# Clustered attention and feed-forward on one core: where transposes, signs, bounds and row sums are computed

## The chip, the core and the metric

The kernel runs on one core of a Trainium2 chip. A core has five engines with instruction queues of their own: TensorE (matrix products into PSUM; PE in the profile, with its weight loads as PEld), VectorE (DVE), ScalarE (ACT), GpSimd (POOL), and SyncE (SP), which issues the transfers of 16 DMA engines. SBUF is the working memory of 128 partitions, PSUM the memory that products are written to, which the kernel divides into named banks. The metric is the device time of one execution in microseconds.

## The reference

```python
def _attn_ref(q, k, v, centroids):            # q, k, v: 4 x 8 x 768 x 64, centroids 8 x 16 x 64
    q_assign = argmax of the cosine of each query with the 16 centroids of its head
    k_assign = the same for the keys
    mask = q_assign[:, :, :, None] == k_assign[:, :, None, :]
    scores = scale * np.matmul(q, k.transpose(0, 1, 3, 2))
    scores = np.where(mask, scores, -1000000000.0)
    scores = scores - np.max(scores, axis=-1, keepdims=True)
    attn = np.exp(scores)
    attn = attn / (np.sum(attn, axis=-1, keepdims=True) + 1e-09)
    return np.matmul(attn, v)

def _moe_ref(x, w_in, w_out):                 # 3072 x 512, 512 x 2048, 2048 x 512
    h = x @ w_in
    g = np.where(h >= 1, h, np.where(h <= -1, 0.0, (h + 1) ** 2 / 4))
    return g @ w_out
```

The attention output, its heads side by side, is the `x` of the second function. The two weight matrices come as 64-bit floats.

## The kernel before

Float32 accuracy is got from float16 products: an operand is scaled by a power of two and split into a high and a low float16 part, and three of the four products of parts are added up in PSUM.

**Attention.** Each of 4 batches has 4 pairs of heads. For a pair, `kv_load` brings k, q and v; `kv_scale` (line 526) reduces k and q to their largest absolute value per partition on VectorE, adds these up over the partitions on TensorE and derives powers of two from the sum (`to_scale`, line 500); `kq_split` (556) splits k and q into "natural" sets `kn` and `qn`, of which there are two each, and transposes them by DMA; `assign` (572) finds the nearest centroid of each row, writes the assignment as extra columns into the natural sets, and transposes them again, so that a product of the columns adds a penalty to scores of different clusters. The queries are taken in chunks of 256 (three a batch). For a chunk and a head pair there are four tiles of 128 queries by 768 keys (two heads j, two halves t). `at_scores` (705) computes a tile's scores into a PSUM bank and moves them to `sS` in one VectorE pass that also finds the row's bound. `at_soft` (735) takes the exponential on ScalarE, which adds up the rows into `rs`, casts the tile to float16, subtracts on GpSimd to get the low part, and sends both through one DMA transpose into `pT`; after the fourth tile `rr` becomes 1 / (sum + 1e-9). `at_av` (758) spreads `rr` over the partitions by four float32 products with an identity, multiplies the transposed tiles by v, and multiplies the two results on VectorE.

Before step 22 (`early()`, line 422) scores alternate between two banks, bank 0 for t = 0 and bank 1 for t = 1; later all are in bank 0, and bank 1 serves the feed-forward part.

**Feed-forward.** Each matrix comes in 8 blocks. `w_load` brings a block, `w_bits` (825) makes float32 out of the 64-bit words: absolute value of the high words on ScalarE, a shift on VectorE, then the low words' bits merged in (lines 849 to 851), then the sign bits (852 to 854). `w_sum` (858) bounds the block's column sums by TensorE, `w_split` (887) scales and splits. Fourteen of the sixteen blocks go through as one piece (`part is None`), two in halves. `ffn1` (900) and `ffn2` (925) run per chunk of 256 rows and block of 256 hidden columns, with the activation on VectorE and ScalarE between them; the cast and the low part of that activation go into `g`, a ring of two buffers.

**Order.** Nothing is issued directly. A recorder takes every operation with a step number, its price (`price`, line 75) and the memory regions it touches (`regions`, 54), simulates the five queues forward and backward for eight rounds, and issues the best order found. In the forward pass an engine may wait for a more urgent operation that becomes ready within `LOOK` times the cost of the one at hand, if it is more urgent by `MARGIN` (182). All recorded instructions have line 289 in the profile, so groups are told apart by tile: `w`, `wk` (weights), `kvq` (k, q, v and their transposes), `am` (bounds), `sS`, `hl`, `pT` (a score tile, its parts, its transpose), `rr`, `rs`, `banka` (products with v, and the spread rows).

Of the kernel before, what the change touches and what calls it, by code (L numbers as in the profile page):

```python
# [20 lines left out]


ONE, ES_MIN = 65504.0, 2.0**-23
EXP_MASK2 = 0x7F000000
TINY = 2.0**-47
W_TINY = 2.0**-90
# [2 lines left out]
LATENCY = dict(tensor=280, scalar=252, vector=230, gpsimd=175)  # L29
COLD, AHEAD = 75e3, 1500  # L30

LOOK, MARGIN = 1.0, 3000
ROUNDS = 8


# [1 line left out]
class Recorder:  # L37
# [15 lines left out]
    @staticmethod  # L53
    def regions(ap):
        if ap.space == bass.MemoryType.DRAM:
            return ap.tensor.name, [(0, 1, 0, 1)]
        size = mybir.dt.size(ap.dtype)
        (row, n), *free = ap.ap
        p0 = ap.start_partition()
        lo = (ap.offset - p0 * row) * size  # L60
        parts = [lo]
        if ap.space == PSUM and len(free) == 2:
            (st, k), *free = free
            parts = [lo + i * st * size for i in range(k)]
        size *= sum((k - 1) * st for st, k in free) + 1
        return ap.tensor.name, [(p0, p0 + n, x, x + size) for x in parts]
# [8 lines left out]
    def price(self, eng, op, out, ins, kw):  # L75

        if "dma" in op:
            n = 1
            for k in out.shape:
                n *= k  # L80
            kb = n * mybir.dt.size(out.dtype) / 1024

            return 33, 79.0 if kb == 2 else kb, "transpose" in op
        n = max(self.free(a) for a in [out] + ins[:1])
        ps = any(a.space == PSUM for a in ins)
        cols = sum(isinstance(kw.get(k), bass.AP) for k in ("scale", "bias", "scalar", "scalar1", "scalar2"))
        if eng == "tensor":
            n = self.free(ins[1])
            half = self.free(ins[0]) <= 64 and n > 100
            if ins[1].dtype == F32:  # L90
                n *= 4
            return n / 4.8 + 1.2 if half else max(n / 2.4 + 2.5, 24)
        if eng == "scalar":
            cols += kw.get("accum_out") is not None
            first = n == 1 and kw.get("scale") == 0.0
            return 93 + n / 1.2 + 94 * cols - 43 * ps + 1283 * first
        if eng == "vector":
            wide = [a for a in ins if self.free(a) > 1 or n == 1]
            wait = 400 if not ps and (len(wide) > 1 or op in ("tensor_scalar", "tensor_copy")) else 0
            fast = 1  # L100
            if op in ("tensor_scalar", "tensor_copy") and not ps:
                fast = 4 if mybir.dt.size(out.dtype) == 2 and mybir.dt.size(ins[0].dtype) == 2 and n > 64 else 2
            return 68 + n / 0.96 / fast + 61 * cols + 20 * (op == "reciprocal") + wait
        return 55 + n * (2.03 if op == "tensor_tensor" else 0.9 if op == "memset" else 3.5)
# [243 lines left out]
def tile_clustered_attention_moe(  # L348
# [10 lines left out]
    nc = tc.nc  # L359
# [50 lines left out]
    wk = tiles("wk", 2, 4096)  # L410
    rings["w32"], rings["x"] = Ring(wk[:1]), Ring(tiles("x", 3, 4096) + wk)

    wb = tiles("w", 1, 2 * NF * 4096)[0]
    raws = [wb[:, (2 * NF - n) * 1024 : (2 * NF - n + 2) * 1024] for n in (2, 4, 6)]
    bank = [psum.tile([P, 1024], F32, name=f"bank{i}") for i in range(3)]
# [21 lines left out]
    rings["c"] = Ring([rings["sS"].bufs[1][:, i * D : (i + 1) * D] for i in range(3)])  # L437
    rings["c_hl"] = Ring([rings["sS"].bufs[2]])
    make_identity(nc, idf)
    iota = const.tile([P, C], F32, name="iota")  # L440
    for c in range(C):
        nc.gpsimd.memset(iota[:, c : c + 1], float(C - c))
    zero = const.tile([P, 1], F32, name="zero")
    nc.gpsimd.memset(zero, 0.0)
    onh = const.tile([P, P], F16, name="onh")
    nc.gpsimd.memset(onh, 1.0)
    ones = const.tile([P, P], BF16, name="ones")
    nc.gpsimd.memset(ones, 1.0)
    cst = new("c", [D], F32)
# [68 lines left out]
    def kv_load(b, hp):  # L518
# [3 lines left out]
        for a, src, n in (("k", k, 1), ("q", q, 2), ("v", v, 3)):  # L522
            st = e[a] = view(e["parts"][n], [2, T * D], F32)
            rec.sync.dma_start(st, heads(src, b, hp))

    def kv_scale(b, hp):
        e = KV[b, hp]
        am = new("am", [2], BF16, 2)
        rec.vector.tensor_reduce(out=am, in_=e["kq"], op=ALU.max, axis=AX.X, apply_absolute_value=True)


        ar = misc(4)
        rec.tensor.matmul(ar[:, :2], ones, am, start=True, stop=True)
        sc = new("sc", [2], F32, 2)
        to_scale(ar[:, :2], sc)


        es, ph = new("es", [1], F32, 2), new("phi", [1], F32, 2)
        raw, ri = ar[:, 2:3], ar[:, 3:4]
        rec.vector.tensor_scalar(  # L540
            out=raw, in0=ar[:, 0:1], scalar1=ar[:, 1:2], scalar2=-QK, op0=ALU.mult, op1=ALU.mult
        )
        rec.vector.tensor_scalar(out=es, in0=raw, scalar1=-ES_MIN, scalar2=None, op0=ALU.min)
        rec.vector.reciprocal(ri, es)
        rec.vector.tensor_scalar(out=ph, in0=raw, scalar1=ri, scalar2=None, op0=ALU.mult)
        e.update(sc=sc, es=es, phi=ph)
# [9 lines left out]
    def kq_split(b, hp):  # L556

        e = KV[b, hp]
        for x, lower, at in (("k", 0, 0), ("q", 1, 4)):
            nat = e[x + "n"] = new(x + "n", [2 * T, 2, D], F16, 2)  # L560
            src = e[x].rearrange("p j (t d) -> p (j t) d", d=D)
            col = "kq".index(x)
            split(nat[:, :, 1 - lower], nat[:, :, lower], src, e["sc"][:, col : col + 1])
            e[x + "T"] = view(e["parts"][at], [2 * T, P], F16)
            transpose(e[x + "T"], nat)
# [6 lines left out]
    def assign(b, hp):  # L572
# [52 lines left out]
        pn = misc(2, C)  # L625
        with rec.group():
            for t in range(T):
                rec.tensor.matmul(pn, onh, kn[:, t::T, 0, :C], start=(t == 0), stop=(t == T - 1))
        has = new("has", [2, C], F32)
        rec.vector.tensor_scalar(out=has, in0=pn, scalar1=-ONE * (S - 0.5), scalar2=None, op0=ALU.is_gt)  # L630

# [73 lines left out]
    def at_scores(b, hp, c, j, t):  # L705
        e = KV[b, hp]
        n = j * CT + t
        pS = view(bank[n % 2 if early() else 0], [2, 512], F32)
        with rec.group():
            for a, (x, y) in enumerate((("qT", "kT"), ("q1", "k1"))):  # L710
                keys = e[y][:, j * T : (j + 1) * T].rearrange("p t q -> p (t q)")
                for h in range(2):
                    rec.tensor.matmul(
                        pS[:, h, :HS],
                        e[x][:, j * T + c * CT + t],
                        keys[:, h * HS : (h + 1) * HS],
                        start=(a == 0),
                        stop=(a == 1),
                    )
        sS = new("sS", [2, HS], F32, 3)  # L720
        bi = new("sbi", [1], F32, 4)

        rec.vector.tensor_tensor_reduce(
            out=sS,
            in0=pS[:, :, :HS],
            in1=zero.to_broadcast([P, S]),
            scale=e["er"][:, j * T + c * CT + t : j * T + c * CT + t + 1],
            scalar=3.0e38,
            op0=ALU.add,
            op1=ALU.min,  # L730
            accum_out=bi,
        )
        A[b, hp, c, j, t] = (sS, bi)

    def at_soft(b, hp, c, j, t):
        e = A.setdefault((b, hp, c), {})
        n = j * CT + t
        sS, bi = A.pop((b, hp, c, j, t))
        if n == 0:
            e["rs"] = new("rs", [4], F32, 4)  # L740
        if t == 0:
# [2 lines left out]
        rec.scalar.activation(  # L744
            out=sf, in_=sf, func=AF.Exp, bias=bi, scale=-1.0, accum_out=e["rs"][:, n : n + 1]
        )
        hl = new("hl", [2, S], F16, 3)
        rec.scalar.copy(hl[:, 0], sf)
        rec.gpsimd.tensor_tensor(out=hl[:, 1], in0=sf, in1=hl[:, 0], op=ALU.subtract)
        rec.sync.dma_start_transpose(out=e["pT", j][:, :, t, :], in_=hl.rearrange("p a s -> p (a s)"))  # L750
        if n == 3:

            rr = new("rr", [4], F32, 3)
            rec.scalar.activation(out=rr, in_=e["rs"], func=AF.Copy, bias=1e-9)
            rec.vector.reciprocal(rr, rr)
            e["rr"] = rr

    def at_av(b, hp, c):
        u = b * NCH + c
# [2 lines left out]
        pv, rb = bank_a[:, :CQ], bank_a[:, CQ:]  # L762
        with rec.group():
            for t in range(CT):
                for j in range(2):
                    rec.tensor.matmul(
                        rb[j * D : (j + 1) * D, t * P : (t + 1) * P],
                        e["rr"][:, j * CT + t : j * CT + t + 1].to_broadcast([P, D]),
                        idf,
                        start=True,  # L770
                        stop=True,
                    )
            for kc in range(T):
                for i, (va, pa) in enumerate(((0, 0), (0, 1), (1, 0))):
                    for j in range(2):
# [49 lines left out]
    def w_bits(a, f, part=None):  # L825
# [7 lines left out]
        if not w_wide:  # L833
# [15 lines left out]
        rec.vector.scalar_tensor_tensor(  # L849
            out=to, in0=lo, scalar=29, in1=t, op0=ALU.logical_shift_right, op1=ALU.bitwise_or  # L850
        )
        rec.vector.scalar_tensor_tensor(
            out=to, in0=hi, scalar=0x80000000, in1=to, op0=ALU.bitwise_and, op1=ALU.bitwise_or
        )
        if part is None:
            WL[a, f][1] = lo

    def w_sum(a, f, part):

# [27 lines left out]
    def w_split(a, f):  # L887
        t, tf = WL.pop((a, f))
        tf = tf.bitcast(F32)
        w = (w1 if a == 0 else w2)[f]  # L890
        whi, wlo = (w[:, x].rearrange("p a f -> p (a f)") for x in range(2))
        sw = WS.pop((a, f))
# [7 lines left out]
    def ffn1(u, f):  # L900
# [16 lines left out]
        rec.vector.tensor_scalar(out=r, in0=phf, scalar1=e["lo"], scalar2=e["hi"], op0=ALU.max, op1=ALU.min)  # L917
        rec.scalar.activation(out=r, in_=r, func=AF.Square, bias=e["ra"], scale=e["rs"])
        rec.vector.scalar_tensor_tensor(out=r, in0=phf, scalar=e["gs"], in1=r, op0=ALU.mult, op1=ALU.max)
        g = new("g", [2, 2 * CQ], F16, 2)  # L920
        rec.scalar.copy(g[:, 0], r)
        rec.gpsimd.tensor_tensor(out=g[:, 1], in0=r, in1=g[:, 0], op=ALU.subtract)
        F[u, f] = g
# [132 lines left out]
```

## Time and profile before

| | us |
|---|---|
| median of 3 runs | 966.27 |
| lowest, highest | 966.08, 966.28 |
| profiled execution, whole | 964.51 |
| its span, first to last instruction | 962.7 |

In the profile, busy time of an engine is the union of its instructions; idle time before an instruction is put down to whatever released it last. A row of a group reads: line, engine, operation, tile written, tiles read, shapes, count, then busy time, mean ns of one, and idle time with its releasers. In a row of the timeline the first number is the start, the second how long the merged instructions took, and the brackets hold the idle time before. A row of waits gives the total, how often, and the longest. The row of a window gives its length, then each engine's busy time with the number of instructions, the clock granted to TensorE, the DMA engines' share and GB/s.

### The profile page before, as it was taken

What the parts mean: (1) busy time and instruction counts of PE and PEld (TensorE: products, weight loads), DVE (VectorE), ACT (ScalarE), POOL (GpSimd) and SP (SyncE); (2) the same over time, 40 slices, a digit from 0 to 9 for tenths busy, and PEclk for the clock granted to TensorE, in tenths of its full rate; (3) what the DMA queues carried; (4) which work ended last, traced back from release to release, by engine and by line L of the source; (5) the groups of instructions that cost most, each with busy time, mean ns of one, the idle gap of its engine ahead of it and who ended that gap; (6) DMA issues with size and microseconds to landing.
All of it is one profiled execution on the core that took longest, in us unless ns stands there. A gap on an engine that the chain in (4) does not pass through costs nothing.

```text
span 962.7 us, 19220 instructions
## 1 busy us (share of the span) xinstructions
PE 824.1 (86%) x7348; PEld 567.2 (59%) x7348; DVE 639.8 (66%) x1341; ACT 654.8 (68%) x1095; POOL 551.2 (57%) x421
## 2 busy tenths in 40 slices
PE   0335547878999999998988999999989999999998
PEld 0223335555666766675656766776666757767664
DVE  6998986878689865556778665546986554454231
ACT  3676877775667877765767687757777677676332
POOL 1375777574555767663655667656655666656311
PEclk9999779989999999999999999999999999999999
DMA  9998787778589986876789878867999776566100
GB/s 279 263 202 195 175 207 161 164 175 194 125 176 178 169 141 117 170 148 142 173 154 198 145 156 152 166 130 159 209 192 154 139 132 122 108 118 110 34 22 22
DMA packets 426780, 148.68 MB, mean 154 GB/s; under 512 B 403520, under 2 KB 418880, under 8 KB 426688
## 3 DMA queue, kind: packets, MB, share of 16 engines
q1 hardware_dynamic: 426688, 147.46, 75.7%
q8 instruction: 57, 0.93, 0.4%
q14 instruction: 35, 0.29, 0.1%
HBM read 40.40 MB, written 6.29 MB: 49 GB/s over the span
## 4 chain that ended last, share of the span: by engine, by line
PE 67%; DVE 22%; issue 5%; ACT 2%; POOL 2%; DMA 1%; SPq 0%; ACTq 0%; DVEq 0%; POOLq 0%
PE bank L289 47%; PE banka L289 12%; PE bankh L289 9%; DVE w L289 4%; DVE sS L289 4%; DVE bank L289 2%; DVE r L289 2%; DVE wk L289 1%; DVE am L289 1%; DVE qn L289 1%; DVE kn L289 1%; POOL hl L289 1%; DVE kvq L289 1%; DVE mx L289 1%; DMA kvq<-in_v_dram 1%
## 5 line engine op out<-in xcount | busy, mean ns | idle before, releaser
L289 POOL TENSOR_TENSOR hl<-sS,hl 128x768 f16<-128x768 f32 x192 | 330.4, 1725 | 182.5 <-ACT hl L289 103.6
L289 PE MATMUL bank<-w,g 128*128 128x512 f16 x1152 | 273.1, 383 | 0.5 <-DVE o L289 0.5
L289 PEld LDWEIGHTS <-kvq 128*64 128x64 f16 (+1 forms) x3264 | 195.4, 107 | 128.3 <-issue 80.8
L289 PEld LDWEIGHTS <-w 128*128 128x128 f16 x2304 | 224.5, 98 | 66.7 <-issue 25.5
L289 DVE CUSTOM_DVE_ANT_0 sS<-bank,zero,er 128x768 f32<-128x768 f32 x192 | 194.2, 1012 | 93.1 <-PE bank L289 77.0
L289 ACT ACTIVATE sS<-sS,sbi 128x768 f32<-128x768 f32 x192 | 179.2, 933 | 98.8 <-DVE sbi L289 92.8
L289 PE MATMUL bank<-kvq 128*128 128x384 f16 x768 | 164.1, 338 | 47.5 <-DVE sbi L289 42.0
L289 POOL TENSOR_TENSOR g<-r,g 128x512 f16<-128x512 f32 x96 | 115.2, 1200 | 152.7 <-ACT g L289 139.5
L289 PEld LDWEIGHTS <-g 128*128 128x128 f16 x1152 | 111.0, 98 | 122.8 <-issue 10.1
L289 ACT CAST hl<-sS 128x768 f16<-128x768 f32 x192 | 157.4, 825 | 7.4 <-DMA pT<-hl 5.6
L289 PE MATMUL bank<-x,w 128*128 128x256 f16 x1032 | 125.6, 275 | 10.0 <-DVE r L289 4.4
L289 ACT ACTIVATE r<-r,f_ra,f_rs 128x512 f32<-128x512 f32 x96 | 77.8, 811 | 79.4 <-DVE r L289 74.7
L289 PE MATMUL banka<-pT,kvq 128*64 128x256 f16 x1728 | 108.0, 281 | 0.0
L289 DVE TENSOR_SCALAR r<-bank,f_lo,f_hi 128x512 f32<-128x512 f32 x64 | 51.7, 808 | 61.6 <-PE bank L289 45.4
L289 ACT CAST g<-r 128x512 f16<-128x512 f32 x96 | 58.8, 613 | 31.7 <-DVE r L289 24.8
L289 DVE SCALAR_TENSOR_TENSOR r<-bank,f_gs,r 128x512 f32<-128x512 f32 x64 | 48.0, 749 | 30.9 <-ACT r L289 18.7
L289 PE MATMUL bank<-wk,w 128*128 128x256 f16 x504 | 60.1, 272 | 5.9 <-DVE r L289 4.9
L289 PE MATMUL bankh<-x,w 128*128 128x256 f16 x504 | 59.9, 273 | 0.2 <-DVE es L289 0.2
L289 DVE TENSOR_SCALAR r<-bankh,f_lo,f_hi 128x512 f32<-128x512 f32 x32 | 25.9, 809 | 30.8 <-PE bankh L289 24.8
L289 PEld LDWEIGHTS <-ones 128*128 128x128 bf16 x148 | 13.9, 120 | 50.5 <-issue 46.7
L289 POOL TENSOR_TENSOR w<-w 128x1024 f16<-128x1024 f32 x14 | 31.5, 2252 | 14.7 <-ACT w L289 14.7
L289 PE MATMUL bank<-wk,ones 128*128 128x128 bf16 x116 | 13.2, 277 | 29.8 <-DVE wk L289 29.8
(135 smaller groups left out, 840.1 us busy)
## 6 DMA issues: line engine op xcount, KB each, us to landing
w<-in_moe_w_in_dram SPq DMA_DIRECT2D x14, 512.0 KB, 4.9
w<-in_moe_w_out_dram SPq DMA_DIRECT2D x14, 512.0 KB, 4.3
kvq<-in_k_dram SPq DMA_DIRECT2D x16, 384.0 KB, 4.0
kvq<-in_q_dram SPq DMA_DIRECT2D x16, 384.0 KB, 3.7
kvq<-in_v_dram SPq DMA_DIRECT2D x16, 384.0 KB, 4.1
out_dram<-o SPq DMA_DIRECT2D x11, 512.0 KB, 3.4
pT<-hl SPq DMA_TRANSPOSE x192, 4.1
o<-in_v_dram SPq DMA_DIRECT2D x8, 384.0 KB, 3.9
```

What stands on the lines that cost most here:

```text
L289: fn(*args, **kw)
```

## The change

- **First batch partly transposed by TensorE.** In `at_soft`, for tiles with t = 0 before step 22, the exponential's result stays float32, six TensorE transposes write it back into the tile's own score bank, ScalarE copies it to the high part in `pT`, and VectorE subtracts for the low part. The cast, GpSimd's subtraction and the DMA transpose of these tiles fall away.
- **Signs off VectorE.** For the 14 whole blocks the sign merge is replaced by ScalarE's `Sign` of the high words in place and a GpSimd multiplication in `w_split`.
- **Bounds off VectorE.** `kv_scale` sums squares on ScalarE (one `Square` with an accumulator for k, one for q) in place of the reduction for the largest absolute value; the squares themselves go into the natural set as scrap. The scale follows by halving the exponent.
- **Four natural sets** for the first batch: two of their own, one in two `x` buffers, one in the buffers of `g` and `o`; later batches alternate between the first two.
- **Rows of 1 / sum by float16 products.** `rr` is split in two float16 parts by two GpSimd operations of 4 columns, and `at_av` spreads it by eight float16 products with an identity scaled by 2^-10, in place of four float32 products.
- **Shorter waits.** `LOOK` falls from 1.0 to 0.4, `MARGIN` rises from 3000 to 4000 (ns); transposes get a price and PSUM regions of more dimensions are split.

```diff
+UNIT = 2.0**-10
-LOOK, MARGIN = 1.0, 3000
+LOOK, MARGIN = 0.4, 4000
...
-        if ap.space == PSUM and len(free) == 2:
+        if ap.space == PSUM and len(free) > 1:
...
+            if op == "transpose":
+                n *= 2
-            if ins[1].dtype == F32:
+            elif ins[1].dtype == F32:
                 n *= 4
...
+    gb = tiles("g", 1, 4096)[0]
+    rings["g"] = Ring([gb[:, :512], gb[:, 512:]])
+    nats = [tiles(f"n{i}", 2, 3072) for i in range(2)] + [rings["x"].bufs[1:3], [gb] + rings["o"].bufs]
...
+    idu = const.tile([P, P], F16, name="idu")
+    rec.gpsimd.tensor_scalar(out=idu, in0=idf, scalar1=UNIT, scalar2=None, op0=ALU.mult)
-    onh = const.tile([P, P], F16, name="onh")
-    nc.gpsimd.memset(onh, 1.0)
...
+    def natural(b, hp, x):
+        n = b * NP + hp
+        return view(nats[n if b == 0 else n % 2]["kq".index(x)], [2 * T, 2, D], F16)
+
     def kv_scale(b, hp):
         e = KV[b, hp]
-        am = new("am", [2], BF16, 2)
-        rec.vector.tensor_reduce(out=am, in_=e["kq"], op=ALU.max, axis=AX.X, apply_absolute_value=True)
+        am = new("am", [2], F32, 2)
+        for i, x in enumerate("kq"):
+            nat = e[x + "n"] = natural(b, hp, x)
+            junk = nat.rearrange("p n a d -> p (n a d)")[:, : 2 * T * D]
+            rec.scalar.activation(
+                out=junk, in_=e[x].rearrange("p j f -> p (j f)"), func=AF.Square, accum_out=am[:, i : i + 1]
+            )
         ar = misc(4)
-        rec.tensor.matmul(ar[:, :2], ones, am, start=True, stop=True)
+        ah = am.bitcast(BF16).rearrange("p (n a) -> p n a", a=2)[:, :, 1]
+        rec.tensor.matmul(ar[:, :2], ones, ah, start=True, stop=True)
         sc = new("sc", [2], F32, 2)
-        to_scale(ar[:, :2], sc)
+        iv = ar[:, :2]
+        ib = iv.bitcast(U32)
+        rec.vector.tensor_scalar(
+            out=ib, in0=ib, scalar1=EXP_MASK2, scalar2=1, op0=ALU.bitwise_and, op1=ALU.logical_shift_right
+        )
+        rec.vector.tensor_scalar(
+            out=iv, in0=iv, scalar1=2.0 ** (64 - 11), scalar2=TINY * 2.0**-11, op0=ALU.mult, op1=ALU.max
+        )
+        rec.vector.reciprocal(sc, iv)
...
     def at_soft(b, hp, c, j, t):
...
+        pT = e["pT", j]
+        if by_tensor(b, hp, c, j, t):
+            with rec.group():
+                for i in range(T):
+                    to = pS[:, i // 3, i % 3 * P : (i % 3 + 1) * P]
+                    rec.tensor.transpose(to, sf[:, i * P : (i + 1) * P], idf)
+            pt = pS[:, :, :HS].rearrange("p h (n q) -> p h n q", q=P)
+            hi, lo = (pT[:, x * T : (x + 1) * T, t, :].rearrange("p (h n) q -> p h n q", h=2) for x in range(2))
+            rec.scalar.copy(hi, pt)
+            rec.vector.tensor_tensor(out=lo, in0=pt, in1=hi, op=ALU.subtract)
+            at_sums(e, n)
+            return
         hl = new("hl", [2, S], F16, 3)
         rec.scalar.copy(hl[:, 0], sf)
         rec.gpsimd.tensor_tensor(out=hl[:, 1], in0=sf, in1=hl[:, 0], op=ALU.subtract)
...
+    def by_tensor(b, hp, c, j, t):
+        return early() and t == 0
+
+    def at_sums(e, n):
         if n == 3:
-            rr = new("rr", [4], F32, 3)
-            rec.scalar.activation(out=rr, in_=e["rs"], func=AF.Copy, bias=1e-9)
+            rr = e["rs"]
+            rec.scalar.activation(out=rr, in_=rr, func=AF.Copy, scale=UNIT, bias=1e-9 * UNIT)
             rec.vector.reciprocal(rr, rr)
-            e["rr"] = rr
+            rh = e["rr"] = new("rr", [2, 4], F16, 3)
+            rec.gpsimd.tensor_copy(rh[:, 0], rr)
+            rec.gpsimd.tensor_tensor(out=rh[:, 1], in0=rr, in1=rh[:, 0], op=ALU.subtract)
...
             for t in range(CT):
-                for j in range(2):
-                    rec.tensor.matmul(
-                        rb[j * D : (j + 1) * D, t * P : (t + 1) * P],
-                        e["rr"][:, j * CT + t : j * CT + t + 1].to_broadcast([P, D]),
-                        idf,
-                        start=True,
-                        stop=True,
-                    )
+                for a in range(2):
+                    for j in range(2):
+                        n = j * CT + t
+                        rec.tensor.matmul(
+                            rb[j * D : (j + 1) * D, t * P : (t + 1) * P],
+                            e["rr"][:, a, n : n + 1].to_broadcast([P, D]),
+                            idu,
+                            start=(a == 0),
+                            stop=(a == 1),
+                        )
...
     def w_bits(a, f, part=None):
...
-        rec.vector.scalar_tensor_tensor(
-            out=to, in0=hi, scalar=0x80000000, in1=to, op0=ALU.bitwise_and, op1=ALU.bitwise_or
-        )
         if part is None:
-            WL[a, f][1] = lo
+            hf = hi.bitcast(F32)
+            rec.scalar.activation(out=hf, in_=hf, func=AF.Sign)
+            WL[a, f] = [hf, lo]
+        else:
+            rec.vector.scalar_tensor_tensor(
+                out=to, in0=hi, scalar=0x80000000, in1=to, op0=ALU.bitwise_and, op1=ALU.bitwise_or
+            )
...
     def w_split(a, f):
         t, tf = WL.pop((a, f))
         tf = tf.bitcast(F32)
+        if t.dtype == F32:
+            rec.gpsimd.tensor_tensor(out=tf, in0=tf, in1=t, op=ALU.mult)
...
-        g = new("g", [2, 2 * CQ], F16, 2)
+        g = new("g", [2, 2 * CQ], F16)
```

More of the change, by code (lines that the diff above doesn't have):

```diff
@@ L559, in kq_split @@
         for x, lower, at in (("k", 0, 0), ("q", 1, 4)):
-            nat = e[x + "n"] = new(x + "n", [2 * T, 2, D], F16, 2)
+            nat = e[x + "n"]
             src = e[x].rearrange("p j (t d) -> p (j t) d", d=D)
@@ L627, in assign @@
             for t in range(T):
-                rec.tensor.matmul(pn, onh, kn[:, t::T, 0, :C], start=(t == 0), stop=(t == T - 1))
+                rec.tensor.matmul(pn, ones, kn[:, t::T, 0, :C], start=(t == 0), stop=(t == T - 1))
         has = new("has", [2, C], F32)
@@ L732, in at_scores @@
         )
-        A[b, hp, c, j, t] = (sS, bi)
+        A[b, hp, c, j, t] = (sS, bi, pS)
     def at_soft(b, hp, c, j, t):
@@ L737, in at_soft @@
         n = j * CT + t
-        sS, bi = A.pop((b, hp, c, j, t))
+        sS, bi, pS = A.pop((b, hp, c, j, t))
         if n == 0:
@@ L749, in at_soft @@
         rec.gpsimd.tensor_tensor(out=hl[:, 1], in0=sf, in1=hl[:, 0], op=ALU.subtract)
-        rec.sync.dma_start_transpose(out=e["pT", j][:, :, t, :], in_=hl.rearrange("p a s -> p (a s)"))
+        rec.sync.dma_start_transpose(out=pT[:, :, t, :], in_=hl.rearrange("p a s -> p (a s)"))
+        at_sums(e, n)
+    def by_tensor(b, hp, c, j, t):
+        return early() and t == 0
+    def at_sums(e, n):
         if n == 3:
-            rr = new("rr", [4], F32, 3)
-            rec.scalar.activation(out=rr, in_=e["rs"], func=AF.Copy, bias=1e-9)
+            rr = e["rs"]
+            rec.scalar.activation(out=rr, in_=rr, func=AF.Copy, scale=UNIT, bias=1e-9 * UNIT)
             rec.vector.reciprocal(rr, rr)
-            e["rr"] = rr
+            rh = e["rr"] = new("rr", [2, 4], F16, 3)
+            rec.gpsimd.tensor_copy(rh[:, 0], rr)
+            rec.gpsimd.tensor_tensor(out=rh[:, 1], in0=rr, in1=rh[:, 0], op=ALU.subtract)
     def at_av(b, hp, c):
```

## The prediction

> **What bounds the kernel now.** I read the head of the page first: how busy each engine is, and its course over 40 slices of 24 us.
>
> ```profile
> span 962.7 us, 19220 instructions
> ...
> PE 824.1 (86%) x7348; PEld 567.2 (59%) x7348; DVE 639.8 (66%) x1341; ACT 654.8 (68%) x1095; POOL 551.2 (57%) x421
> ...
> PE   0335547878999999998988999999989999999998
> ...
> DVE  6998986878689865556778665546986554454231
> ```
>
> TensorE is busy 9 tenths from the tenth slice on and under half before; VectorE is the opposite. So there are two stages with different limits. The view of windows puts numbers on them.
>
> ```profile
> core 0: us, PE busy (x) PEld busy (x) DVE busy (x) ACT busy (x) POOL busy (x), PEclk, DMA share, GB/s
> 0.00:24.00 24.00, 2.25 (x52) 1.96 (x53) 16.53 (x40) 9.11 (x12) 3.60 (x27) 1.00 0.93 278
> 24.00:144.00 120.00, 53.12 (x487) 35.86 (x487) 110.44 (x224) 87.59 (x121) 77.26 (x46) 0.90 0.90 208
> 144.00:240.00 96.00, 77.72 (x662) 53.41 (x661) 74.30 (x182) 69.56 (x129) 63.00 (x44) 0.94 0.80 174
> 240.00:900.00 660.00, 635.00 (x5750) 439.11 (x5750) 422.46 (x878) 471.14 (x809) 394.87 (x293) 0.99 0.79 150
> 900.00:963.00 63.00, 56.00 (x401) 36.91 (x399) 16.04 (x21) 17.39 (x26) 12.43 (x12) 0.98 0.05 18
> ```
>
> From 24 to 144 us VectorE works 110.4 of 120 us (92%), the DMA engines 90% (108 us), ScalarE 73%, TensorE 44%. From 240 to 900 us TensorE works 635 of 660. TensorE's work is fixed, so the end is that work plus its idle time: 107 us idle before 240 us (240 − 133.1), 25 between 240 and 900, 7 after. A microsecond is won by taking work off TensorE late, or by taking load off VectorE and DMA early.
>
> **The change part by part: rows of 1 / sum (TensorE, all 48 calls).** The timeline of TensorE in the late stage, then one line of weight loads, then a product with 128 columns at two clocks:
>
> ```profile
> 420.95 0.66 PE L289 MATMUL banka<-idf,rr 128*64 128x128 f32 x8
> 421.44 2.14 PE L289 MATMUL banka<-pT,kvq 128*64 128x256 f16 x36
> 423.51 0.39 PE L289 MATMUL bank<-w,g 128*128 128x512 f16 x1
> ...
> 421.44 0.23 PEld L289 LDWEIGHTS <-kvq 128*64 128x64 f16 x4
> ...
> 98.42 1.01 PE L289 MATMUL bank<-wk,ones 128*128 128x128 bf16 x8 [0.24 <-DVE wk L289]
> 122.15 0.62 PE L289 MATMUL bank<-wk,ones 128*128 128x128 bf16 x8 [1.10 <-DVE wk L289]
> ```
>
> Start to start, the float32 group holds TensorE 421.44 − 420.95 = 0.49 us. The float16 group behind it gives 36 products of 256 columns in 2.07 us, 57.5 ns each (two run side by side in the two halves). The change issues 8 float16 products of 128 columns: at half the columns 8 × 28.8 = 0.23 us, so 0.26 us is won per call. Bounds: no less than nothing is won if loading weights sets the pace (four rounds of one 0.11 us load: 0.44 us, 0.05 won); at most 0.27. I take 0.26, the row with the same weights. Nine calls lie before 240 us where TensorE has time; the other 39 give **10.1 us** (2 to 10.5). GpSimd gets two operations of 4 columns per call.
>
> ```profile
> L289 POOL COPY w_all<-w_iw 128x2 f32<-128x2 f32 x8 | 2.5, 307 | 2.4 <-DVE w_iw L289 2.2
> pT<-hl SPq DMA_TRANSPOSE x192, 4.1
> ```
>
> At 0.2 to 0.3 us each (that row) they queue behind a GpSimd subtraction and delay only the product. Cover: the last tile's transpose, which starts after its own subtraction and lands 4.1 us later. Without it each of 39 calls could cost some 0.5 us, 20 us at worst.
>
> [...]
>
> **Signs and bounds off VectorE, part of the transposes on TensorE.** Groups by shape, the first four and the tile reduction for 24 to 144 us, the others for the whole run:
>
> ```profile
> L289 DVE SCALAR_TENSOR_TENSOR w<-w 128x1024 uint32<-128x1024 uint32 x12 | 21.7, 1811 | 0.0
> L289 ACT ACTIVATE wk<-w 128x1024 f32<-128x1024 f32 x12 | 13.4, 1120 | 6.6 <-DVE w L289 5.1 <-issue 1.6
> L289 POOL TENSOR_TENSOR w<-w 128x1024 f16<-128x1024 f32 x11 | 25.1, 2284 | 11.7 <-ACT w L289 11.7
> L289 POOL TENSOR_TENSOR hl<-sS,hl 128x768 f16<-128x768 f32 x18 | 37.5, 2091 | 17.3 <-ACT hl L289 6.5 <-DVE wk L289 6.3 <-DMA w<-in_moe_w_out_dram 4.5
> L289 DVE CUSTOM_DVE_ANT_0 sS<-bank,zero,er 128x768 f32<-128x768 f32 x21 | 21.0, 1009 | 1.5 <-POOL hl L289 1.2
> ...
> L289 DVE TENSOR_REDUCE am<-kvq 128x2 bf16<-128x1536 f32 x16 | 27.9, 1744 | 4.3 <-DMA kvq<-in_k_dram 2.6 <-DMA kvq<-in_q_dram 1.8
> L289 ACT ACTIVATE sS<-sS,sbi 128x768 f32<-128x768 f32 x192 | 179.2, 933 | 98.8 <-DVE sbi L289 92.8 <-POOL wk L289 2.1 <-DVE has L289 1.2
> L289 ACT ACTIVATION_READ_ACCUMULATOR sS<-sS,sbi 128x1 f32 x192 | 35.8, 187 | 0.0
> L289 DVE TENSOR_TENSOR bank<-bank,mx 128x384 f32<-128x384 f32 x24 | 13.5, 562 | 2.4 <-PE bank L289 2.1
> L289 DVE TENSOR_TENSOR rb<-banka,rb 128x256 f32<-128x256 f32 x48 | 20.0, 418 | 19.7 <-ACT rb L289 19.7
> L289 ACT ACTIVATE o<-bank,f_io 128x512 f32<-128x512 f32 x24 | 15.2, 678 | 6.8 <-PE bank L289 6.8
> L289 ACT CAST hl<-sS 128x768 f16<-128x768 f32 x192 | 157.4, 825 | 7.4 <-DMA pT<-hl 5.6
> ```
>
> Eleven tiles take the new way (first query half of a tile pair, steps below 22). In 24 to 144 us:
> - **VectorE**: 12 sign merges go (21.7 us) and one reduction (1.7); eleven subtractions out of PSUM come: (562 − 418) / 128 = 1.1 ns a column, so 562 + 384 × 1.1 = 0.98 us each, 10.8. 110.4 becomes 97.8.
> - **ScalarE**: 12 signs at the 1.12 us of the absolute value over the same strided words (13.4); two squares at 0.93 + 0.19 (2.2); eleven casts (0.83) become copies out of PSUM, about 0.68 + 256 × 0.83 ns = 0.9, 0.8 more. 87.6 becomes 104.0.
> - **GpSimd**: 12 multiplications at 2.28 (27.4) come, eleven subtractions at 2.09 (23.0) go, some 2 us of small ones come: 77.3 becomes 83.7. Each multiplication stands in the place of the merge in the weights' chain, so that chain gains little; behind it queue subtractions for transposes.
> - **TensorE**: 66 transposes. The two rows of 8 bfloat16 products give (0.62 − 0.22) / 7 = 57 ns warm and (1.01 − 0.31) / 7 = 0.1 cold; float32 as an ordinary product, 0.49 us for four that run two by two, about 0.25. So 4 to 16 us, I take 9, beside 67 us of idleness in this window.
> - **DMA**: 11 transposes go. Their size in time:
>
> ```profile
> q1 hardware_dynamic: 426688, 147.46, 75.7%
> ...
> HBM read 40.40 MB, written 6.29 MB: 49 GB/s over the span
> ```
>
> The queue took 0.757 × 962.7 = 729 us; plain traffic (46.7 MB, at the 0.93 × 24 us for 6.7 MB of the first window, 3.3 us a MB) is 155 of it; 574 over 257 transposes (192, four for each of 16 head pairs, one) is 2.2 us each. 108 becomes 83. On SP's queue eleven issues go too, so the loads and transposes behind them start earlier.
>
> The busiest goes from 110.4 (VectorE) to 104.0 (ScalarE). Packed like VectorE now (92%), the window shrinks to 113: 7 us. In VectorE's proportion it would be 106: 14 us; with ScalarE in the chain, 0. I take **8**. Before 24 us three reductions (5.2 us) leave a VectorE chain without gaps from 10 us on, while DMA stays at 93%: **2.5** (0 to 5). The four sets remove waits for transposes there and in the next tens of us; they are within these sums. A square now writes into a natural set, so from the second batch on it waits for that set's transposes of two head pairs earlier, many us old by then: nothing. The new identity and the dropped ones are single small GpSimd operations in the first 3 us, where GpSimd works 3.6 of 24: nothing. From 144 to 240 us two merges, a reduction and four product groups: **2** (0 to 6).
>
> **Bounds, late.** Eleven of the 16 reductions lie after 240 us. TensorE's longest named waits there:
>
> ```profile
> PE bank L289 <- DVE r L289: 11.4, 10, 3.5
> PE bank L289 <- DVE sbi L289: 7.3, 8, 1.4
> ```
>
> Both are evictions that stood behind something on VectorE. 19 us come off it; ScalarE gets 25, in pieces of 1.1, at 71% busy. I take **3** (8 won to 4 lost).
>
> **Shorter waits of the planner** (0.4 of an operation's cost, 4 us margin), with its new prices, reorder everything a little. VectorE idles only 9.6 us in 24 to 144 and TensorE 25 later, so 5 us either way; I take 0.
>
> **Sum**: 10.1 + 8 + 2.5 + 2 + 3 = 25.6. The profiled run took 964.5 (span 962.7 and 1.8 around it): 938.9. The median of the runs, 966.3, lies 1.8 above that run: 940.7, so **941 us**.
>
> **Rivals.**
> 1. ScalarE takes VectorE's place early (104 against 98 us of work, and its exponential releases both the TensorE transposes and the cast): stage gain nil. 966.3 − 10.1 − 3 = **953**. For it: 27% idle before is what it spends. Against: its waits are for VectorE. Chance 0.15.
> 2. Weight loads pace the new row products: 2 instead of 10 us, **949**. Chance 0.10.
> 3. Slower: **bank 0 held too long**. Now a tile's scores free the bank after VectorE's pass; for eleven tiles it is then held through exponential, transposes, ScalarE copy and subtraction. Behind it on TensorE's queue stand the next scores for that bank.
>
> ```profile
> 45.75 1.00 DVE L289 CUSTOM_DVE_ANT_0 sS<-bank,zero,er 128x768 f32<-128x768 f32 x1
> 79.88 1.44 PE L289 MATMUL bank<-kvq 128*128 128x384 f16 x4 [1.46 <-DVE bank L289]
> PE bank L289 <- DVE sbi L289: 24.9, 12, 3.4
> ```
>
>    21 tiles in 45.8 to 144 us make 4.7 us a tile, 9.4 a pair, and each pair needs bank 0 once. The hold is 1.44 + 1.01 + 1.12 + 0.8 + 0.9 + 0.98 = 6.3 us, and five handovers. With 0.6 us each it fits; the early queues are full, and TensorE already waits for VectorE's pass here (24.9 us in 12 waits). It eats the whole gain when a hold is 9.4 + 25.6 / 11 = 11.7 us; at 12.2 the cost is 11 × 2.8 = 31, **972**. Chance 0.08.
> 4. Sign changes ScalarE's table:
>
> ```profile
> L289 ACT ACT_TABLE_LOAD x2 | 2.6, 1283 | 0.7 <-PEq L1039 0.7
> ```
>
>    Now two loads serve everything. If sign isn't in the exponential's table, 14 signs need 28 loads, 36 us on ScalarE; 31 of them in the window make 135 us of work in 120, 15 us late instead of 8 early: **964**. Chance 0.03. [...]
>
> **How the numbers follow.** All steps as worked out: 0.64. Early (0 to 25, taken 12.5), late bounds (8 won to 4 lost, taken 3) and planner (5 either way) are independent; the root of the sum of their squares is some 14 either way, 927 to 955. Rivals 1 and 2 lie at 953 and 949 with a spread of their own, so the range is **927 to 960**; rivals 3 and 4 and the tails stay outside. 0.2% is 2 us, about what runs of this kernel can tell apart. Faster 0.87, same 0.03, slower 0.10.
>
> **What would show it.** In the profile after: float16 row products starting under 0.25 us ahead of the value products; VectorE near 98 us in the first 135 and ScalarE above it; first score pass before 43 us (now 45.75); two table loads; TensorE near 820 us busy (824.1 − 14 + 9). Wrong would be: long TensorE or VectorE waits for the eleven transposed tiles, ScalarE over 95% early, or GpSimd's small operations ending TensorE's waits.

## The result, and the profile after

The changed kernel takes 921.67 us (median of four runs, 919.56 to 923.2) against 966.27: a ratio of 0.9535, 95% interval 0.951 to 0.9561, or 44.6 us less. Forecast were 941 us and a range of 927 to 960; the time lies 5 us under the range.

The head of the page of the kernel after (recorded instructions have line 292 there):

```profile
span 921.4 us, 19471 instructions
...
PE 812.9 (88%) x7414; PEld 559.2 (61%) x7414; DVE 604.1 (66%) x1322; ACT 691.6 (75%) x1173; POOL 565.6 (61%) x520
...
PE   0256668988998999999989999998998999999998
...
DVE  5998777887888565646776665547886555554222
...
ACT  6989997977778677778868778777887677777232
```

TensorE reaches 9 tenths in the eighth slice and stays near it from the tenth on; from 24 to 144 us ScalarE has taken VectorE's place as the busiest engine (109.3 against 101.9 us below). The view of windows, with the columns of before's and the last bound moved to where the last products with v stand now (860 us; 900 before):

```profile
0.00:24.00 24.00, 2.68 (x30) 2.30 (x31) 13.30 (x38) 15.46 (x22) 5.56 (x27) 1.00 0.96 293
24.00:144.00 120.00, 66.21 (x653) 46.44 (x650) 101.87 (x235) 109.29 (x153) 85.62 (x66) 0.87 0.83 197
144.00:240.00 96.00, 86.19 (x802) 59.93 (x801) 79.87 (x205) 78.25 (x145) 69.39 (x60) 1.00 0.81 170
240.00:860.00 620.00, 602.89 (x5549) 414.51 (x5546) 393.05 (x824) 471.25 (x829) 392.86 (x357) 1.00 0.82 155
860.00:921.40 61.40, 54.91 (x393) 36.08 (x392) 16.03 (x21) 17.39 (x26) 12.19 (x11) 0.99 0.05 18
```

The span is TensorE's work plus its idle time, so the 41.3 us that the span lost split in three. Work: 824.1 to 812.9, **11.2**. Idle time before 240 us: 106.9 to 240 − 155.1 = 84.9, **22.0**. Idle time after 240 us: 962.7 − 824.1 − 106.9 = 31.7 to 17.1 + 6.5 = 23.6, **8.1**. The forecast had, in the same terms, 5 less work, and 20 less idle time early and late together.

Groups by shape of the kernel after, whole run:

```profile
L292 ACT ACTIVATE n<-kvq 128x768 f16<-128x768 f32 x28 | 23.3, 833 | 4.4 <-DMA kvq<-in_k_dram 3.5 <-DMA kvq<-in_q_dram 0.6 <-DMA kvq<-n 0.2
L292 PE MATMUL banka<-idu,rr 128*64 128x128 f16 x384 | 20.5, 230 | 0.0
L292 ACT ACTIVATE w<-w 128x1024 f32<-128x1024 f32 x14 | 15.9, 1139 | 0.0
...
L292 PE MATMUL bank<-idf,sS 128*128 128x128 f32 x66 | 12.6, 341 | 14.9 <-ACT sS L292 12.7 <-POOL w L292 2.2
L292 POOL CAST rr<-rs 128x4 f16<-128x4 f32 x48 | 11.5, 239 | 10.9 <-DVE rs L292 10.9
L292 POOL TENSOR_TENSOR rr<-rs,rr 128x4 f16<-128x4 f32 x48 | 10.5, 218 | 3.2
L292 DVE TENSOR_TENSOR pT<-bank,pT 128x768 f16<-128x768 f32 x11 | 10.5, 951 | 1.8 <-ACT pT L292 1.8
...
L292 ACT CAST pT<-bank 128x768 f16<-128x768 f32 x11 | 8.7, 791 | 0.1
```

From the top: the squares, the row products, the signs, the 66 transposes by TensorE, GpSimd's two small operations, and the subtraction and copy out of PSUM. Most new operations take about what the nearest row of before had said: a sign 1.14 us (1.12 forecast), a subtraction out of PSUM 0.95 (0.98), a copy 0.79 (0.9), a square 0.83 (0.93), a small GpSimd operation 0.22 to 0.24 (0.2 to 0.3). (The 0.83 ns a column in the copy's forecast agree with the casts of before: 825 ns for 768 columns, 613 for 512, so 212 / 256.) The 66 transposes take 12.6 us where 9 were taken (4 to 16; the rows of products that the prediction calls warm and cold lie where the granted clock was 1.00 and 0.50), and TensorE sits idle 14.9 us ahead of them, 12.7 of it until the exponential is done; all of this lies before 240 us.

### The profile page after: what moved, and what is told of

Read it like the earlier page. It is cut to its first block, busy times and chain, and to the rows that moved or that the text cites. A ratio compares the mean times of both kernels' runs of the same rounds, so it can differ in the third digit from the quotient of the medians.

```text
span 921.4 us, 19471 instructions
## 1 busy us (share of the span) xinstructions
PE 812.9 (88%) x7414; PEld 559.2 (61%) x7414; DVE 604.1 (66%) x1322; ACT 691.6 (75%) x1173; POOL 565.6 (61%) x520
## 4 chain that ended last, share of the span: by engine, by line
PE 65%; DVE 10%; ACT 6%; issue 5%; POOL 3%; ACTq 0%; DVEq 0%; POOLq 0%
PE bank L292 47%; PE banka L292 10%; PE bankh L292 8%; DVE sS L292 3%; DVE r L292 2%; ACT sS L292 2%; DVE bank L292 2%; POOL hl L292 1%; ACT w L292 1%; DVE bankh L292 1%; DVE mx L292 1%; ACT hl L292 1%; POOL g L292 1%; ACT r L292 1%; DVE n L292 0%
## 5 line engine op out<-in xcount | busy, mean ns | idle before, releaser
L292 POOL TENSOR_TENSOR hl<-sS,hl 128x768 f16<-128x768 f32 x181 | 303.9, 1683 | 148.7 <-ACT hl L292 115.9
L292 PEld LDWEIGHTS <-kvq 128*64 128x64 f16 (+1 forms) x3264 | 191.1, 106 | 86.2 <-issue 41.3
L292 POOL TENSOR_TENSOR g<-r,g 128x512 f16<-128x512 f32 x96 | 112.6, 1173 | 122.8 <-ACT g L292 119.2
L292 PE MATMUL bank<-kvq 128*128 128x384 f16 x768 | 162.4, 336 | 19.3 <-DVE sbi L292 14.1
L292 ACT CAST hl<-sS 128x768 f16<-128x768 f32 x181 | 148.3, 825 | 4.9 <-DMA pT<-hl 3.7
L292 POOL TENSOR_TENSOR w<-w 128x1024 f32<-128x1024 f32 (+1 forms) x28 | 59.8, 2143 | 33.9 <-ACT w L292 32.0
L292 ACT CAST g<-r 128x512 f16<-128x512 f32 x96 | 58.8, 612 | 25.2 <-DVE r L292 18.7
L292 PEld LDWEIGHTS <-ones 128*128 128x128 bf16 x244 | 17.2, 107 | 53.5 <-issue 38.5
L292 ACT ACTIVATE n<-kvq,sc 128x768 f16<-128x768 f32 x42 | 37.1, 924 | 1.7 <-DVE sc L292 1.6
```

Source lines behind the costliest of these rows:

```text
L292: fn(*args, **kw)
```

## The experiments

Two theories were put against each other. By the first each part, or one of them, is worth more than I gave it, and undoing it shows how much. (The expectations call this P; W, E and R are forms of it that put the surplus on the waiting rule, the early parts or the row products.) By the second (L) the parts are worth about what was forecast, and the rest comes from **the order** that the planner happened to find: every edit makes it issue another order. The numbers below are medians; ratios are to the kernel before, run on the same chip beside each, with 95% intervals. The runs lie on several chips, on which the median of before was 961.8 to 966.7, so a difference of two medians from different chips can be some 5 us off. "Costs" is the difference to 921.7.

**The row products and the waiting rule, undone in after and done alone in before.**

e1_old_waits (after):

```diff
-LOOK, MARGIN = 0.4, 4000
+LOOK, MARGIN = 1.0, 3000
```

> The changed kernel with the planner's old waiting rule (1.0 of an operation's cost, 3000 ns margin). Theory W (the 19 us missing from the forecast are the waiting rule, which was priced at nothing): 935 to 945. Theory E (the early parts were priced at half their worth, the rule is worth nothing): 918 to 926.

932.0 us, 0.967 (0.9638 to 0.9701): the old rule costs 10.4.

e2_f32_rows (after, the four float32 products and `rr` as before):

```diff
-            rh = e["rr"] = new("rr", [2, 4], F16, 3)
...
+            e["rr"] = rr
...
+                        e["rr"][:, j * CT + t : j * CT + t + 1].to_broadcast([P, D]),
+                        idf,
```

> The changed kernel with the rows of 1 / sum by float32 products again. Both theories W and E keep the forecast term of 10 us for the late calls (39 x 0.24 us measured start to start in the trace): 929 to 935. A third theory R (the rows were worth more than their TensorE time, since the early calls run at half clock and GpSimd's order changes): above 938.

946.6 us, 0.982 (0.9782 to 0.9858): it costs 24.9. (What R says of the early calls holds for some of them. Ahead of 240 us, five of before's nine take 0.90 to 0.91 us from start to start in place of 0.49, four of these at a granted clock of 0.50 and the first at 1.00; in after three of ten take 0.43 in place of 0.25, all at 0.50.)

e7_before_new_waits (before):

```diff
-LOOK, MARGIN = 1.0, 3000
+LOOK, MARGIN = 0.4, 4000
```

> The kernel before with nothing but the new waiting rule (0.4, 4000 ns). Theory W: 945 to 952. Theory E: 964 to 968. If the order is a lottery of its own (theory L), anything from 955 to 978.

960.2 us, 0.9959 (0.994 to 0.9978): the rule wins some 4 here.

e8_before_f16_rows (before, with the new `rr`, `idu` and row products; `ones` takes the place of `onh`):

```diff
+            rh = e["rr"] = new("rr", [2, 4], F16, 3)
+            rec.gpsimd.tensor_copy(rh[:, 0], rr)
+            rec.gpsimd.tensor_tensor(out=rh[:, 1], in0=rr, in1=rh[:, 0], op=ALU.subtract)
```

> The kernel before with nothing but the float16 rows of 1 / sum. Forecast term: 10 us off, 954 to 958. Theory R: below 952. If weight loads set the pace: 963 to 966.

953.4 us, 0.9892 (0.9851 to 0.9933): the rows win some 10 here, and undoing them costs 25 there. TensorE's work differs less. The head of the pages of e8 and e2, two fences:

```profile
PE 810.4 (85%) x7348; PEld 556.1 (59%) x7348; DVE 636.6 (67%) x1341; ACT 656.4 (69%) x1095; POOL 561.7 (59%) x517
```

```profile
PE 829.5 (88%) x7414; PEld 575.3 (61%) x7414; DVE 607.3 (64%) x1322; ACT 694.2 (74%) x1173; POOL 548.3 (58%) x424
```

The float16 rows take 824.1 − 810.4 = 13.7 us of work off TensorE in the one pair and 829.5 − 812.9 = 16.6 in the other. So the 25 us of e2 don't look like the rows' alone: some 8 are not TensorE's work.

**The early parts, each undone in after.**

e3_dma_transposes:

```diff
     def by_tensor(b, hp, c, j, t):
-        return early() and t == 0
+        return False
```

> The changed kernel with all tile transposes by DMA again. Theory E (the early parts together are worth some 25 us instead of 12.5, shared among them): 926 to 934. If the eleven transposes only moved work to a fuller ScalarE and held bank 0 (rival 3 in a mild form): 917 to 922. Theory L (single parts shift the order, and the order decides by 10 us and more): outside both.

939.0 us, 0.9729 (0.9699 to 0.9758): costs 17.4.

e4_signs_dve (`w_bits`; the multiplication in `w_split` falls away with it):

```diff
+        rec.vector.scalar_tensor_tensor(
+            out=to, in0=hi, scalar=0x80000000, in1=to, op0=ALU.bitwise_and, op1=ALU.bitwise_or
+        )
...
-            rec.scalar.activation(out=hf, in_=hf, func=AF.Sign)
```

> The changed kernel with the sign bits merged on VectorE again: 26 us back on VectorE, 16 off ScalarE, 29 off GpSimd. Theory E: 928 to 936, the largest of the early parts. If ScalarE is the early bound now: 916 to 921. Theory L: outside both.

939.2 us, 0.9731 (0.9699 to 0.9762): costs 17.6.

e5_bounds_dve (`kv_scale`):

```diff
-                out=junk, in_=e[x].rearrange("p j f -> p (j f)"), func=AF.Square, accum_out=am[:, i : i + 1]
...
+        rec.vector.tensor_reduce(out=am, in_=e["kq"], op=ALU.max, axis=AX.X, apply_absolute_value=True)
...
+        to_scale(ar[:, :2], sc)
```

> The changed kernel with the bounds of k and q by the VectorE reduction again (16 of 1.74 us). Forecast terms (2.5 early, 3 late): 925 to 929. Theory E: 926 to 932. Theory L: outside both.

946.8 us, 0.9815 (0.9783 to 0.9847): costs 25.2.

e6_two_sets (`natural`):

```diff
-        return view(nats[n if b == 0 else n % 2]["kq".index(x)], [2 * T, 2, D], F16)
+        return view(nats[n % 2]["kq".index(x)], [2 * T, 2, D], F16)
```

> The changed kernel with two natural sets in the first batch too. Forecast: nothing of its own, 919 to 925. If the two sets keep the first head pairs behind their transposes: 928 to 940. Theory L: anything from 915 to 945.

934.7 us, 0.9687 (0.966 to 0.9714): costs 13.0.

Added up, the six undoings in after cost 10.4 + 24.9 + 17.4 + 17.6 + 25.2 + 13.0 = 108 us, where the whole change won 44.6. Parts that overlap can give such a sum, but so does an order that any edit spoils. Against the expectations: e1 (932.0) lies between its two ranges and e8 (953.4) between the forecast and R; e3, e4 and e5 lie above every range that prices a part, which only L allowed; e7 (960.2) lies in L's range alone, e2 where R put it, and e6 in two ranges. The next runs tell more.

**Other orders of the same operations.** The planner's simulation adds a fixed latency per engine to each hand-over. One or two nanoseconds more or less there change nothing that is computed and no operation, only which of two nearly equal choices the planner takes. In after:

```diff
-LATENCY = dict(tensor=280, scalar=252, vector=230, gpsimd=175)
+LATENCY = dict(tensor=280, scalar=253, vector=230, gpsimd=175)
```

is s1_after_scalar253. s2 and s9 set `vector` to 231 and 229, and s3 takes 2 off all four.

> The changed kernel, its operations untouched; only ScalarE's latency in the planner's model is 253 instead of 252 ns, which reorders the queues. Theory L (any new order lands some 10 us either way, and the changed kernel's order is a lucky one): 928 to 942. Theory P (each part is worth what its undoing cost): 918 to 926, since no part is touched.

> The changed kernel, only VectorE's latency in the planner's model 231 instead of 230 ns. Theory L: 928 to 942. Theory P: 918 to 926.

> The changed kernel, all four latencies of the planner's model 2 ns lower; the planner's own span is the lowest of all versions (890.7 against 892.6 us). Theory L: 925 to 940, whatever the planner says. Theory P: 916 to 924.

> The changed kernel, VectorE's latency in the planner's model 229 ns. Theory L, by the three reorderings so far (mean 935, spread 7): 925 to 945. Theory P: 918 to 926.

942.7 us (0.9776, 0.9738 to 0.9813), 928.3 (0.9627, 0.9588 to 0.9666), 934.7 (0.9691, 0.9657 to 0.9725) and 930.6 (0.9636, 0.9603 to 0.9668). All four lose, by 6.6 to 21.0 us, with no operation touched; the largest of these losses is above four of the six undoings. So undoing one part by itself says little of what it is worth. Three of the four lie in the range that L gave; s1 is 0.7 us above it.

The windows of s1, and its longest waits of TensorE (total, times, longest), then those waits of after:

```profile
24.00:144.00 120.00, 64.24 (x618) 45.82 (x618) 110.41 (x225) 104.89 (x148) 82.07 (x60) 0.84 0.86 197
144.00:240.00 96.00, 80.64 (x659) 53.30 (x658) 74.23 (x200) 75.95 (x141) 66.53 (x57) 0.95 0.70 144
240.00:860.00 620.00, 594.77 (x5537) 409.68 (x5535) 389.17 (x824) 467.38 (x822) 388.89 (x357) 1.00 0.84 156
```

```profile
PE bank L292 <- DVE sbi L292: 22.1, 21, 2.7
...
PE bank L292 <- DVE r L292: 11.1, 13, 1.3
PE bank L292 <- DVE pT L292: 8.1, 6, 2.9
```

```profile
PE bank L292 <- DVE sbi L292: 15.4, 15, 3.0
...
PE bank L292 <- DVE r L292: 7.5, 11, 1.4
...
PE bank L292 <- DVE pT L292: 3.6, 4, 2.1
```

The loss has no single place: 5.5 us of TensorE's work are missing from 144 to 240 us, 8.1 from 240 to 860, and the same three waits behind VectorE are each some 3.5 to 7 us longer in sum. That fits an order that moves evictions to other places in VectorE's queue; no run moves one of them alone.

**The same for before, and for a kernel without the early parts.** In before, s4 sets `scalar` to 253, s5 `vector` to 229, s6 takes 2 off all.

> The kernel before, only ScalarE's latency in the planner's model 253 instead of 252 ns. If the kernel before is an ordinary order with the spread of the changed kernel's reorderings (9 us): 955 to 975. If it is an unlucky one, below 955.

> The kernel before, only VectorE's latency in the planner's model 229 instead of 230 ns (the planner's span is 0.6 us shorter). Ordinary: 955 to 975. Unlucky before: below 955.

> The kernel before, all four latencies of the planner's model 2 ns lower (planner's span 3.5 us longer). Ordinary: 955 to 978. Unlucky before: below 955.

941.6 us (0.9781, 0.9757 to 0.9806), 945.5 (0.9825, 0.9803 to 0.9848) and 958.7 (0.9956, 0.9937 to 0.9975). All three win: one nanosecond in the planner's table is worth 20 us to the old kernel (961.8 to 941.6 on one chip), nearly half of what the whole change brought. The page and a window of s4:

```profile
span 939.7 us, 19214 instructions
...
PE 818.7 (87%) x7348; PEld 566.4 (60%) x7348; DVE 638.2 (68%) x1341; ACT 654.4 (70%) x1095; POOL 553.6 (59%) x421
```

```profile
240.00:860.00 620.00, 604.43 (x5555) 420.94 (x5553) 406.98 (x842) 454.64 (x784) 379.42 (x283) 1.00 0.83 156
```

Its late stage is as full as after's (604.4 of 620 against 602.9), with VectorE still doing all its old work.

e9_no_early is after with the edits of e3, e4, e5 and e6 together; it keeps the float16 rows and the new rule. s7 is e9 with `scalar` at 253, s8 with `vector` at 231.

> The changed kernel without its early parts: transposes by DMA, signs and bounds on VectorE, two natural sets; it keeps the float16 rows and the new waiting rule. Theory P, adding what the undoings cost (17 + 18 + 25 + 13 over 922): above 970. Theory L with early parts worth the forecast 15 us together: 940 to 955. Theory E (early parts worth about 30): 945 to 958.

> The version without the early parts, ScalarE's latency in the planner's model 253 ns (planner's span 6.5 us longer than at 252). If 943.5 is an ordinary order of it: 935 to 955. If the early parts are worth 25 us and more, 943.5 is a lucky order and this is above 955.

> The version without the early parts, VectorE's latency in the planner's model 231 ns (planner's span 3.7 us longer than at 230). Early parts worth the forecast 15 us over a mean of some 932 for the changed kernel: 938 to 956. Worth 25 and more: above 956.

943.5 us (0.9786, 0.9753 to 0.9819), 959.4 (0.9968, 0.9951 to 0.9984) and 942.4 (0.9758, 0.9735 to 0.9782). Here too one nanosecond is worth some 16 us. (s7 alone lies where its expectation put early parts worth 25 us and more; e9 and s8 lie where they are worth about 15.) Two pages and windows, e9's first and then s7's, show the same early stage (55 us of TensorE's work in both) and another late one (599 against 590):

```profile
span 941.8 us, 19265 instructions
```

```profile
24.00:144.00 120.00, 55.36 (x521) 36.86 (x521) 104.95 (x222) 88.84 (x123) 80.52 (x56) 0.69 0.97 212
...
240.00:860.00 620.00, 599.27 (x5558) 413.00 (x5556) 411.52 (x849) 459.07 (x796) 395.69 (x359) 0.99 0.83 158
```

```profile
span 956.2 us, 19283 instructions
```

```profile
24.00:144.00 120.00, 55.18 (x477) 34.35 (x478) 103.56 (x219) 84.58 (x115) 75.83 (x53) 0.70 0.91 201
...
240.00:860.00 620.00, 589.99 (x5460) 405.21 (x5459) 406.94 (x848) 445.77 (x771) 385.80 (x353) 0.99 0.81 154
```

**Kinds compared, orders averaged.** With several orders of each kind the parts can be told from the order. From each page (span, TensorE's work) and its window 0 to 240 us (240 less TensorE's work there); the idle time late is the rest of the span:

| kind (orders) | times, us | mean | TensorE's work | idle before 240 | idle after 240 |
|---|---|---|---|---|---|
| before (before, s4, s5, s6) | 966.3, 941.6, 945.5, 958.7 | 953.0 | 821.2 | 102.1 | 27.6 |
| no early parts (e9, s7, s8) | 943.5, 959.4, 942.4 | 948.4 | 811.1 | 105.1 | 30.0 |
| after (after, s1, s2, s3, s9) | 921.7, 942.7, 928.3, 934.7, 930.6 | 931.6 | 816.7 | 85.8 | 27.8 |

Orders of one kind scatter with a standard deviation of 11.5, 9.5 and 7.8 us (rough values, from three to five orders). So the means are good to 5.7, 5.5 and 3.5, and a difference of two to 7 or 8. TensorE's work scatters less (2.5 to 5.0), and so does its idle time before 240 us (2.8 to 4.6). By the means the change is worth **21 us** with an ordinary order (14.5 if the two originals are left out: 948.6 against 934.1). The early parts, with the late bounds among them, bring 16.8 of it, by 19.3 less idle time before 240 us and 2.2 less after at 5.6 more work. The rows and the rule together bring 4.6, by 10.1 less work and 5 more idle time; that net isn't told apart from nothing. By the means of the ratios (0.989, 0.984, 0.965), which leave out what differs between chips, the change is worth 2.4%, some 23 us, and the early parts 1.8%, some 18. One rival stays untried: the clock granted to TensorE from 24 to 144 us was 0.86 to 0.91 in the orders of before, 0.69 to 0.71 without the early parts and 0.84 to 0.88 in those of after, so a part of both differences may be the clock's.

The other 23 of the 44.6 are the two orders: the one shown as before lies 13.3 above the mean of its kind, the one shown as after 9.9 below its own. That before lies above its kind and after below is luck of the two orders, as far as the runs show. None of the other versions was faster than after.

## Why the prediction was wrong, point by point

- **What bounds the kernel: right.** The gain is TensorE's work and its idle time, most of it early, in the terms that the prediction named. The course of TensorE was read loosely: 7 to 8 tenths stand from the seventh slice of before to the tenth, and 9 from the eleventh; the sums went by the windows, where this makes no difference.
- **Rows of 1 / sum: right.** In the timeline of TensorE after, the row products start 0.24 us ahead of the products with v:

```profile
411.13 0.41 PE L292 MATMUL banka<-idu,rr 128*64 128x128 f16 x8
411.37 2.13 PE L292 MATMUL banka<-pT,kvq 128*64 128x256 f16 x36
```

  Over the last 39 calls the starts lie 19.0 us apart in sum before and 9.6 after: 9.4 won, 10.1 forecast. Rival 2 (weight loads set the pace) is false: it would have made 0.44 us a call. The loads of the 64 columns overlap: each one here is recorded with 105 to 110 ns, yet eight of the row products and 36 of the products with v are through in 0.25 and 1.92 us:

```profile
411.12 0.25 PEld L292 LDWEIGHTS <-rr 128*64 128x64 f16 x8 [0.21 <-issue]
411.32 1.92 PEld L292 LDWEIGHTS <-kvq 128*64 128x64 f16 x36
```

  By the kinds the 10.1 us of work went, but with the rule only 4.6 ± 8 of it is seen in the time. GpSimd's two operations stayed under cover in after: no wait of TensorE for `rr` is listed there.
- **The early window: right in size, as far as the kinds tell; the road is open.** Forecast for the early parts and the late bounds, which the kinds hold together, were 8 + 2.5 + 2 + 3 = 15.5 us; 16.8 ± 7 is what the kinds differ by. As forecast, ScalarE passes VectorE (109.3 against 101.9 us; 104.0 and 97.8 were worked out). Rival 1 (ScalarE takes over and nothing is won) is false: it is 91% busy, and the stage still gains. All ten versions with TensorE's transposes idle 81.4 to 92.3 us before 240 us, all ten without 98.7 to 108.3. e3, which has every other early part, is among the latter with 99.7. That points to the transposes, but their own 12.6 us are work put into that idle time, the clock in e3 is lower too (0.72 against 0.87), and e3 is one order; how the gain splits among the parts stays open.
- **First score pass before 43 us: wrong.** The timeline of VectorE after:

```profile
55.52 1.00 DVE L292 CUSTOM_DVE_ANT_0 sS<-bank,zero,er 128x768 f32<-128x768 f32 x1
```

  It is 9.8 us later than before, not 3 earlier: the new order takes weight blocks first (six have the low words' bits merged in by then, three before). The first product of `ffn1` comes at 140.1 us instead of 154.2 all the same. That a milestone's direction could turn with the order wasn't in the prediction.
- **Bank 0 held too long (rival 3): false.** The wait that would show it, behind the new subtraction, is 3.6 us in four waits. (The 14.9 us that TensorE idles ahead of the transposes are another wait, for the exponential. The prediction named long waits for these tiles as a sign of being wrong; these lie where TensorE idled 106.9 us before, and no run shows that they cost time.) **Sign changes the table (rival 4): false.** The two table loads of after are those at the start:

```profile
0.73 1.28 ACT L292 ACT_TABLE_LOAD   x1 [0.73 <-PEq L1093]
...
6.56 1.28 ACT L292 ACT_TABLE_LOAD   x1
```

- **Bounds, late: not told apart.** TensorE's waits after 240 us fell in after:

```profile
PE bank L292 <- DVE r L292: 5.5, 9, 1.3
PE bank L292 <- DVE sbi L292: 4.5, 5, 1.5
```

  Together 10.0 against 18.7 in the rows of before, while the wait behind the row `bank` rose from 1.3 to 4.2. The idle time after 240 us is 27.6 and 27.8 in the kinds of before and after: the 3 us forecast are not seen there. And s4, which has the old bounds, has as full a late stage, so that fall needs no new bounds.
- **The step that failed: "Shorter waits of the planner … reorder everything a little … so 5 us either way; I take 0".** Zero was a fair middle, and 5 was the mis-sized term. I read it from the idle time that was left: VectorE's 9.6 us early and TensorE's 25 late. The runs show 8 to 11.5 us of standard deviation for one order, so some 12 to 14 for the difference of two, and here both orders fell on the side of the gain. The idle time before 240 us, where TensorE had 107 us to lose or win, belonged in that bound. With a deviation of 13, the bound that holds 8 times in 10 is 17; in place of the 5 it makes the prediction's 14 some 21 (14² − 5² + 17² = 21.4²), and the range begins near 920. The forecast of 25.6 us itself agrees with the kinds (21 ± 7), which says more of the sum than of each term.

Not settled: what the new waiting rule is worth by itself (−4 us in e7, 10 to undo in e1, both within the scatter), what the clock did to the kinds, and whether the two orders were luck alone or something that the edits favour.

## What to carry to other kernels

Where a planner writes the order, an edit is timed together with a new order: time several orders of the same operations, on both sides, before a difference of one or two per cent is put down to the edit. Undoing one part of a fast version can measure above all how good its order was; averages over orders, or steadier quantities such as TensorE's work and its idle time in a stage, tell more. In a forecast, the reordering has a term of its own, as wide as such orders scatter, and trying neighbouring orders can be worth as much as the edit.

## What was not expected of the hardware

- How much of the time is order alone: with identical operations 921.7 to 942.7 and 941.6 to 966.3 us, while the runs of one kernel lie within some 7 us, all chips taken together.
- The clock granted to TensorE from 24 to 144 us was 0.69 to 0.72 in the five versions with float16 rows and without TensorE's transposes (e3, e8, e9, s7, s8), and 0.84 to 0.91 in the others but e4 (0.74) and e7 (0.79). TensorE's busy time doesn't tell them apart: without transposes it was 52 to 56 us of 120 at the low clock and 53 to 58 in before, s4, s5, s6 and e7. Why was not tried; the transposes may win some of their time there.
- The 64-column weight loads of the row products cost no time of their own that shows: eight products in 0.24 us, 30 ns each.
